# Transposes directly behind the next scores, and readers of matmul results one slot later, in a bucketed attention with a gated feed-forward

## The chip, the core and the metric

The kernel runs on one NeuronCore of a Trainium2 chip. Its engines work side by side: TensorE (PE for matmuls, PEld for the loads of their stationary operand), VectorE (DVE), ScalarE (ACT), GpSimd (POOL) and SyncE (SP), which issues the DMA transfers here. In the trace each of them runs its instructions in the order in which the program lists them, so one that has to wait holds up those behind it on its engine. The metric is the device time of one execution in microseconds (us).

## The reference

There are 4 batches, 8 heads, 768 positions and 64 elements per head. Each query and key gets a bucket from the signs of six projections, and a query attends only to keys of its own bucket. The outputs of the heads are laid side by side to 512 columns and go through a feed-forward with a causal convolution as gate.

```
q_bits = (np.einsum('bhsd,dk->bhsk', q, proj) > 0)      # keys alike
mask = q_bucket[:, :, :, None] == k_bucket[:, :, None, :]
scores = np.where(mask, scale * q @ k.T, -1e9)
attn = exp(scores - max) / sum;   x = attn @ v           # heads merged: B, S, 512
gate = sigmoid(sum_k conv_w[k] * xp[:, k:k + S, :])      # five taps
out = (gate * (x @ w_val)) @ w_out
```

## The kernel before

A unit is one head of one batch; there are 32. A unit has six tiles of 128 queries, so there are 192 tiles, and the main loop runs over them: slot `k` is one turn of that loop. The instruction order of TensorE, VectorE, ScalarE and GpSimd is the order of the code (`manual_schedule`).

A tile goes through the slots as a pipeline. `scores(k + 1)` in slot k multiplies the queries with all 768 keys (four matmuls, L266; the bucket comparison is part of the product through extra rows) into one of two pairs of PSUM banks, `s`. `maxima(k)`, `factors(k)` and `shifts(k)` on VectorE (L272, L278, L282) find the row's maximum and from it the scale and shift of the exponential. `exponentials(k)` on ScalarE (L290) writes `p` and the row's sum; it frees the banks that `scores(k + 2)` needs. In each even slot VectorE inverts the sums of two tiles (`row_sums`, `recip`), which waits for the exponential of the later one. `normalise(k - 2)` on GpSimd (L305) scales `p`. `transposes(k - 3)` turns it over in two halves of three matmuls each (L314) into two banks `tp`, and `keep_transposed` copies each half to SBUF as `pt` on ScalarE (L323), at the start of the next slot.

When the six tiles of a unit are done, `attn_v` multiplies them with the values into the single bank `av` (L337): two key blocks, that is four matmuls, in each odd slot, and so three odd slots for a unit. At its end ScalarE copies `av` to `x` (L345, two copies), and for every second unit `pair_x` splits `x` and runs the convolution's taps (L357 to L368). When a batch has its four pairs, four sigmoids follow (L372), and `moe` becomes the batch's feed-forward, a generator that the loop advances by about a step per slot. A step is four matmuls. Three steps fill one accumulator: either a `val` (L399), which VectorE multiplies with the gate (L404, `ht`) and then splits (L408, L410), or an `outp` (L424), which ScalarE or VectorE copies to `o` (L432, L430) for the output DMA. In the loop the accumulator is the single bank `m`; after the loop `tp` and `s` serve as well.

In the first third of the loop VectorE, ScalarE and GpSimd also convert the weights (L91 to L113), and TensorE computes bucket projections ahead (L204, L226), which VectorE reads at once (L207, L229).

In slot k TensorE's order is: scores of tile k + 1, a step of the feed-forward, bucket projections if any, value products if k is odd, transposes of tile k - 3. ScalarE's is: copies of the transposes of tile k - 4, exponential of tile k, then the readers of results that came in this slot.

Of the kernel before, what the change touches and what calls it, by code (L numbers as in the profile page):

```python
# [8 lines left out]
FP32 = mybir.dt.float32  # L9
FP32R = mybir.dt.float32r  # L10
AF = mybir.ActivationFunctionType
ALU = mybir.AluOpType
# [14 lines left out]
def kernel(  # L27
# [10 lines left out]
    nc = tc.nc  # L38
    B, H, _, S = qk.shape
    P = 128  # L40
    D = 64
    KB = S // P
    HS = S // 2
    NP = H // 2
    KW = 5
    LAG = 3
# [11 lines left out]
    xp = ctx.enter_context(tc.tile_pool(name="xp", bufs=2))  # L58
# [269 lines left out]
    def attn_v(i, pts):  # L328
        b, h = units[i]
        hh, c = h % 2, h // 2  # L330
        av = ps_v.tile([P, 512], FP32, name="av")
        vt = vts[i]
        for kb in range(KB):
            if kb:
                yield
            for s, pt in enumerate(pts):
                nc.tensor.matmul(out=av[s * D:(s + 1) * D, 0:HS], lhsT=vt[:, kb, hh * D:(hh + 1) * D], rhs=pt[kb // 3][:, kb % 3, :],  # L337
                                 start=(kb == 0), stop=(kb == KB - 1), tile_position=(0, s * D))
        if hh == 0:
            x = cur["x"] = xp.tile([P, S + KW - 1], FP32, name="x")  # L340
            nc.gpsimd.memset(x[:, 0:KW - 1], 0.0)
        x = cur["x"]
        for s in range(2):
            o = KW - 1 + s * HS
            nc.scalar.copy(out=x[hh * D:(hh + 1) * D, o:o + HS], in_=av[s * D:(s + 1) * D, 0:HS])  # L345
        if hh == 1:
            if c == 0:
                cur["xs"], cur["g"] = {}, []
            convs.append(pair_x(b, c, x, cur["g"], cur["xs"]))

    def pair_x(b, c, x, gs, xs_):
        for o in (0, HS):
# [21 lines left out]
            moes.append(moe(b, xs_, gs))  # L374

    def acc_tile():
        pools = accs
        pool, name = pools[0]
        pools.append(pools.pop(0))
        if name == "s":  # L380
            return pool.tile([P, 2, 512], FP32, name="s")[:, 0, :]
        return pool.tile([P, 512], FP32, name=name)

    def moe(b, xs_, g):
# [7 lines left out]
        def val(o, j):  # L392
            acc = acc_tile()
            m = 0
            for wi, xi in ((0, 0), (1, 0), (0, 1)):
                if m:
                    yield
                for c in range(NP):
                    nc.tensor.matmul(out=acc[:, 0:HS], lhsT=wv[wi][:, c, j * P:(j + 1) * P],  # L399
                                     rhs=xs_[(c, o)][xi], start=(m == 0), stop=(m == 11))  # L400
                    m += 1
                later()
            ht = hp.tile([P, HS], FP32, name="ht", bufs=2)
            nc.vector.tensor_tensor(out=ht, in0=acc[:, 0:HS], in1=g[j][:, o:o + HS], op=ALU.mult)  # L404

            def split():
                hh = hp.tile([P, HS], FP32R, name="hh")
                nc.vector.tensor_copy(out=hh, in_=ht)  # L408
                hl = hp.tile([P, HS], FP32R, name="hl")
                nc.gpsimd.tensor_tensor(out=hl, in0=ht, in1=hh.bitcast(FP32), op=ALU.subtract)  # L410
                hs[(o, j)] = (hh, hl)
            todo.append(split)
            yield

        def outp(o, tb):
            for gens in weights:
                finish(gens)
            acc = acc_tile()
            m = 0
            for hi, wi in ((0, 0), (0, 1), (1, 0)):  # L420
                if m:
                    yield
                for j in range(NP):
                    nc.tensor.matmul(out=acc, lhsT=hs[(o, j)][hi][:, tb * P:(tb + 1) * P],  # L424
                                     rhs=wo[wi][:, j, :], start=(m == 0), stop=(m == 11))
                    m += 1
                later()
            ob = op.tile([P, 512], FP32, name="o")
            if cur["gates"]:
                nc.vector.tensor_copy(out=ob, in_=acc)  # L430
            else:
                nc.scalar.copy(out=ob, in_=acc)  # L432
            r0 = o + tb * P
            nc.sync.dma_start(out=out[b, r0:r0 + P, :], in_=ob)
            yield

        def idle(n):
# [18 lines left out]
    tiles = [(i, qt) for i in range(len(units)) for qt in range(KB)]  # L456

    raws, stacks, vts, ss, nbs, ps, tps, sums, rcs, nms, gs, cur = {}, {}, {}, {}, {}, {}, {}, {}, {}, {}, {}, {}
    avs, convs, moes, early = [], [], [], {}
    accs = [(ps_m, "m")]  # L460

    def step(gens):
# [7 lines left out]
    def finish(gens):  # L470
        while gens:
            step(gens)
# [3 lines left out]
    with tc.manual_schedule(engines=ENGINES):  # L476
# [10 lines left out]
        step(weights[1])  # L487
        ahead = [early_bits()]
        turn = 0
        for k in range(N + LAG + 1):  # L490
            if 0 <= k - LAG - 1:
                keep_transposed(k - LAG - 1)
            pair = k % 2 == 0 and 0 <= k - 2 < N
            if k < N:
                maxima(k)
# [14 lines left out]
                scores(k + 1)  # L510
            if k < N:
                exponentials(k)
            if k >= 60 or k % 2:
                step(convs)
            for _ in range((1, 0, 2, 0, 2, 2)[k % 6]):
# [10 lines left out]
            if k % 2:  # L526
                step(avs)
                step(avs)
            if 0 <= k - LAG < N:
                transposes(k - LAG)  # L530
        accs[:] = [(ps_m, "m"), (ps_t, "tp"), (ps_s, "s"), (ps_t, "tp"), (ps_s, "s")]
        finish(avs)
        cur["gates"] = 0
        cur["end"] = True
        while convs:
# [62 lines left out]
```

## Time and profile before

| | |
|---|---|
| median of 3 runs | 622.93 us (622.74 to 623.79) |
| span of the profiled execution, first to last instruction | 620.8 us |
| instructions | 10648 |
| TensorE matmuls busy | 585.5 us, 94% |
| VectorE busy | 437.6 us, 70% |
| ScalarE busy | 421.4 us, 68% |
| GpSimd busy | 395.6 us, 64% |

The profiled execution is one run; its time is its span, and the runs' times are taken around it on the device, so that the median stands 2.1 us over the span. A busy share is a mean over the whole span, and stages with different limits are mixed in it. The matmuls are pipelined and their ends are modelled, so that two of them overlap in the listing.

### The profile page before, as it was taken

What the parts mean: (1) busy time and instruction counts of PE and PEld (TensorE: products, weight loads), DVE (VectorE), ACT (ScalarE), POOL (GpSimd) and SP (SyncE); (2) the same over time, 40 slices, a digit from 0 to 9 for tenths busy, and PEclk for the clock granted to TensorE, in tenths of its full rate; (3) what the DMA queues carried; (4) which work ended last, traced back from release to release, by engine and by line L of the source; (5) the groups of instructions that cost most, each with busy time, mean ns of one, the idle gap of its engine ahead of it and who ended that gap; (6) DMA issues with size and microseconds to landing.
All of it is one profiled execution on the core that took longest, in us unless ns stands there. A gap on an engine that the chain in (4) does not pass through costs nothing.

```text
span 620.8 us, 10648 instructions
## 1 busy us (share of the span) xinstructions
PE 585.5 (94%) x3496; PEld 423.4 (68%) x3496; DVE 437.6 (70%) x1017; ACT 421.4 (68%) x881; POOL 395.6 (64%) x373
## 2 busy tenths in 40 slices
PE   5789898989999999999999999999999999999997
PEld 2655565555657777776767777777667877775895
DVE  5869798998975866668575867569665877665532
ACT  2777777778778666777787676777787766765400
POOL 3576868778766765578564777568764777544321
PEclk9799999999999999999999999999999999999999
DMA  6467666564532235243433234333422213200111
GB/s 227 123 197 199 200 167 208 157 175 118 133 83 68 70 79 142 72 108 82 122 82 107 61 80 126 84 115 82 108 70 78 67 42 91 69 18 1 51 52 51
DMA packets 29031, 64.64 MB, mean 104 GB/s; under 512 B 4937, under 2 KB 10057, under 8 KB 28977
## 3 DMA queue, kind: packets, MB, share of 16 engines
q1 hardware_dynamic: 28832, 63.93, 37.8%
q8 instruction: 28, 0.46, 0.3%
q14 instruction: 27, 0.21, 0.1%
q10 hardware_dynamic: 144, 0.03, 0.0%
HBM read 30.60 MB, written 7.86 MB: 62 GB/s over the span
## 4 chain that ended last, share of the span: by engine, by line
PE 66%; DVE 12%; ACT 12%; DMA 5%; issue 3%; POOL 2%; SPq 1%; ACTq 0%; POOLq 0%; DVEq 0%
PE av L337 17%; PE s L266 16%; PE tp L314 12%; PE m L424 8%; PE m L399 7%; ACT p L290 5%; DVE nm L272 4%; ACT pt L323 3%; ACT x L345 2%; DMA w<-in_w_val_dram 2%; DVE g L368 2%; PE tp L399 1%; PE tp L424 1%; PE s L424 1%; DMA bk<-bq 1%
## 5 line engine op out<-in xcount | busy, mean ns | idle before, releaser
L305 POOL TENSOR_SCALAR p<-p,ri 128x768 f32<-128x768 f32 x192 | 210.5, 1100 | 156.0 <-DVE nb L282 130.8
L272 DVE TENSOR_REDUCE nm<-s 128x1 f32<-128x768 f32 x192 | 182.5, 950 | 61.2 <-PE s L266 61.0
L290 ACT ACTIVATE p<-s,nb,gs 128x768 f32<-128x768 f32 x192 | 192.6, 1003 | 46.2 <-DVE nb L282 41.9
L323 ACT COPY pt<-tp 128x384 f32<-128x384 f32 x384 | 165.7, 485 | 75.3 <-PE tp L314 74.4
L314 PEld LDWEIGHTS tp<-ident,p 128*128 128x128 f32 x1152 | 130.3, 142 | 72.2 <-issue 43.6
L314 PE MATMUL tp<-ident,p 128*128 128x128 f32 x1152 | 164.4, 279 | 2.6 <-ACT pt L323 2.1
L337 PE MATMUL av<-pt,vt 128*64 128x384 f32 x768 | 144.9, 498 | 0.0
L266 PE MATMUL s<-ak,aq 76*128 76x384 f32 x384 | 118.1, 389 | 23.2 <-ACT p L290 19.7
L266 PE MATMUL s<-bk,bq 128*128 128x384 f32 x384 | 101.3, 345 | 0.4 <-DVE bq L252 0.4
L337 PEld LDWEIGHTS av<-pt,vt 128*64 128x64 f32 x768 | 47.0, 136 | 61.5 <-issue 61.4
L266 PEld LDWEIGHTS s<-ak,aq 76*128 76x128 f32 x384 | 59.2, 194 | 38.7 <-ACT p L290 34.6
L368 DVE SCALAR_TENSOR_TENSOR g<-x,cw_sb,g 128x768 f32<-128x768 f32 x64 | 79.4, 1241 | 2.2 <-POOL g L366 2.1
L266 PEld LDWEIGHTS s<-bk,bq 128*128 128x128 f32 x384 | 71.7, 194 | 0.8 <-issue 0.8
L173 POOL TENSOR_TENSOR bq<-r,aq 128x768 fp32r<-128x768 f32 x31 | 59.2, 1909 | 0.1
L410 POOL TENSOR_TENSOR hl<-ht,hh 128x384 fp32r<-128x384 f32 x32 | 32.3, 1009 | 39.5 <-DVE hh L408 39.5
L345 ACT COPY x<-av 64x384 f32<-64x384 f32 x64 | 30.4, 475 | 29.7 <-PE av L337 29.0
L282 DVE TENSOR_SCALAR nb<-nm,gs 128x1 f32<-128x1 f32 x192 | 40.4, 211 | 3.5
L399 PE MATMUL m<-xh,wv 128*128 128x384 f32 x200 | 42.7, 337 | 0.0
L358 POOL TENSOR_TENSOR xl<-x,xh 128x384 fp32r<-128x384 f32 x32 | 33.4, 1059 | 13.8 <-DVE xh L357 13.8
L290 ACT ACTIVATION_READ_ACCUMULATOR p<-s,nb,gs 128x1 f32 x192 | 39.0, 203 | 0.0
L404 DVE TENSOR_TENSOR ht<-m,g 128x384 f32<-128x384 f32 x25 | 13.9, 556 | 35.6 <-PE m L399 29.2
L424 PE MATMUL m<-wo,hh 128*128 128x512 f32 x144 | 38.1, 394 | 0.0
(86 smaller groups left out, 486.9 us busy)
## 6 DMA issues: line engine op xcount, KB each, us to landing
r<-in_qk_dram SPq DMA_DIRECT2D x32, 384.0 KB
vt<-in_v_dram SPq DMA_DIRECT2D x16, 384.0 KB
out_dram<-o SPq DMA_DIRECT2D x24, 256.0 KB
ak<-aq SPq DMA_DIRECT2D x31, 192.0 KB
bk<-aq SPq DMA_DIRECT2D x31, 192.0 KB
bk<-bq SPq DMA_DIRECT2D x31, 192.0 KB
bq<-aq SPq DMA_DIRECT2D x31, 192.0 KB
hh<-in_qk_dram SPq DMA_DIRECT2D x16, 192.0 KB
```

The source lines that it names most:

```text
L173: nc.gpsimd.tensor_tensor(out=bq, in0=r, in1=aq.bitcast(FP32), op=ALU.subtract)
L266: nc.tensor.matmul(out=s[:, hf, 0:HS], lhsT=lq[0:n, qs], rhs=rk[0:n, hf * HS:(hf + 1) * HS], start=n == M, stop=n == P)
L272: nc.vector.tensor_reduce(out=nm, in_=s[:, :, 0:HS], axis=AX.XY, op=ALU.max, negate=True)
L290: nc.scalar.activation(out=p, in_=s[:, :, 0:HS], func=AF.Exp, bias=nb, scale=gs.pop(k), accum_out=sm[:, k % 2, 0:1])
L305: nc.gpsimd.tensor_scalar(out=p, in0=p, scalar1=rcs.pop(k), scalar2=1.0, op0=ALU.mult, op1=ALU.mult)
L314: nc.tensor.transpose(out=tp[:, n * P:(n + 1) * P], in_=p[:, kb * P:(kb + 1) * P], identity=ident)
L323: nc.scalar.copy(out=pt[:, :, qo:qo + P], in_=tp[:, 0:HS].rearrange("p (a b) -> p a b", b=P))
L337: nc.tensor.matmul(out=av[s * D:(s + 1) * D, 0:HS], lhsT=vt[:, kb, hh * D:(hh + 1) * D], rhs=pt[kb // 3][:, kb % 3, :], start=(kb == 0), s ...
L345: nc.scalar.copy(out=x[hh * D:(hh + 1) * D, o:o + HS], in_=av[s * D:(s + 1) * D, 0:HS])
L368: nc.vector.scalar_tensor_tensor(out=g, in0=x[:, k:k + S], scalar=w, in1=g, op0=ALU.mult, op1=ALU.add)
L399: nc.tensor.matmul(out=acc[:, 0:HS], lhsT=wv[wi][:, c, j * P:(j + 1) * P], rhs=xs_[(c, o)][xi], start=(m == 0), stop=(m == 11))
L424: nc.tensor.matmul(out=acc, lhsT=hs[(o, j)][hi][:, tb * P:(tb + 1) * P], rhs=wo[wi][:, j, :], start=(m == 0), stop=(m == 11))
```

## The change

The copy of `av` to `x`, the gating of a `val` and the store of an `outp` become closures. They are put on a list, `readers`, which is emptied in the next slot right after the exponential of that slot, or when the next accumulator is taken; after the loop they run at once. The transposes move from the end of the slot to the place behind the exponential in the code, which on TensorE is directly behind the scores, and their copies follow in the same slot. The loop is one slot shorter.

```diff
--- before.py
+++ after.py
@@ -336,17 +336,29 @@
             for s, pt in enumerate(pts):
                 nc.tensor.matmul(out=av[s * D:(s + 1) * D, 0:HS], lhsT=vt[:, kb, hh * D:(hh + 1) * D], rhs=pt[kb // 3][:, kb % 3, :],
                                  start=(kb == 0), stop=(kb == KB - 1), tile_position=(0, s * D))
-        if hh == 0:
-            x = cur["x"] = xp.tile([P, S + KW - 1], FP32, name="x")
-            nc.gpsimd.memset(x[:, 0:KW - 1], 0.0)
-        x = cur["x"]
-        for s in range(2):
-            o = KW - 1 + s * HS
-            nc.scalar.copy(out=x[hh * D:(hh + 1) * D, o:o + HS], in_=av[s * D:(s + 1) * D, 0:HS])
-        if hh == 1:
-            if c == 0:
-                cur["xs"], cur["g"] = {}, []
-            convs.append(pair_x(b, c, x, cur["g"], cur["xs"]))
+
+        def take():
+            if hh == 0:
+                x = cur["x"] = xp.tile([P, S + KW - 1], FP32, name="x")
+                nc.gpsimd.memset(x[:, 0:KW - 1], 0.0)
+            x = cur["x"]
+            for s in range(2):
+                o = KW - 1 + s * HS
+                nc.scalar.copy(out=x[hh * D:(hh + 1) * D, o:o + HS], in_=av[s * D:(s + 1) * D, 0:HS])
+            if hh == 1:
+                if c == 0:
+                    cur["xs"], cur["g"] = {}, []
+                convs.append(pair_x(b, c, x, cur["g"], cur["xs"]))
+        soon(take)
+
+    def soon(f):
+        readers.append(f)
+        if cur["end"]:
+            read()
+
+    def read():
+        while readers:
+            readers.pop(0)()
 
     def pair_x(b, c, x, gs, xs_):
         for o in (0, HS):
@@ -374,6 +386,7 @@
             moes.append(moe(b, xs_, gs))
 
     def acc_tile():
+        read()
         pools = accs
         pool, name = pools[0]
         pools.append(pools.pop(0))
@@ -401,7 +414,10 @@
                     m += 1
                 later()
             ht = hp.tile([P, HS], FP32, name="ht", bufs=2)
-            nc.vector.tensor_tensor(out=ht, in0=acc[:, 0:HS], in1=g[j][:, o:o + HS], op=ALU.mult)
+
+            def gate():
+                nc.vector.tensor_tensor(out=ht, in0=acc[:, 0:HS], in1=g[j][:, o:o + HS], op=ALU.mult)
+                todo.append(split)
 
             def split():
                 hh = hp.tile([P, HS], FP32R, name="hh")
@@ -409,7 +425,7 @@
                 hl = hp.tile([P, HS], FP32R, name="hl")
                 nc.gpsimd.tensor_tensor(out=hl, in0=ht, in1=hh.bitcast(FP32), op=ALU.subtract)
                 hs[(o, j)] = (hh, hl)
-            todo.append(split)
+            soon(gate)
             yield
 
         def outp(o, tb):
@@ -425,13 +441,16 @@
                                      rhs=wo[wi][:, j, :], start=(m == 0), stop=(m == 11))
                     m += 1
                 later()
-            ob = op.tile([P, 512], FP32, name="o")
-            if cur["gates"]:
-                nc.vector.tensor_copy(out=ob, in_=acc)
-            else:
-                nc.scalar.copy(out=ob, in_=acc)
-            r0 = o + tb * P
-            nc.sync.dma_start(out=out[b, r0:r0 + P, :], in_=ob)
+
+            def store():
+                ob = op.tile([P, 512], FP32, name="o")
+                if cur["gates"]:
+                    nc.vector.tensor_copy(out=ob, in_=acc)
+                else:
+                    nc.scalar.copy(out=ob, in_=acc)
+                r0 = o + tb * P
+                nc.sync.dma_start(out=out[b, r0:r0 + P, :], in_=ob)
+            soon(store)
             yield
 
         def idle(n):
@@ -456,7 +475,7 @@
     tiles = [(i, qt) for i in range(len(units)) for qt in range(KB)]
 
     raws, stacks, vts, ss, nbs, ps, tps, sums, rcs, nms, gs, cur = {}, {}, {}, {}, {}, {}, {}, {}, {}, {}, {}, {}
-    avs, convs, moes, early = [], [], [], {}
+    avs, convs, moes, early, readers = [], [], [], {}, []
     accs = [(ps_m, "m")]
 
     def step(gens):
@@ -487,9 +506,7 @@
         step(weights[1])
         ahead = [early_bits()]
         turn = 0
-        for k in range(N + LAG + 1):
-            if 0 <= k - LAG - 1:
-                keep_transposed(k - LAG - 1)
+        for k in range(N + LAG):
             pair = k % 2 == 0 and 0 <= k - 2 < N
             if k < N:
                 maxima(k)
@@ -510,6 +527,10 @@
                 scores(k + 1)
             if k < N:
                 exponentials(k)
+            read()
+            if 0 <= k - LAG < N:
+                transposes(k - LAG)
+                keep_transposed(k - LAG)
             if k >= 60 or k % 2:
                 step(convs)
             for _ in range((1, 0, 2, 0, 2, 2)[k % 6]):
@@ -526,10 +547,9 @@
             if k % 2:
                 step(avs)
                 step(avs)
-            if 0 <= k - LAG < N:
-                transposes(k - LAG)
         accs[:] = [(ps_m, "m"), (ps_t, "tp"), (ps_s, "s"), (ps_t, "tp"), (ps_s, "s")]
         finish(avs)
+        read()
         cur["gates"] = 0
         cur["end"] = True
         while convs:
```

On TensorE, in the feed-forward of the first batch (`s` scores, `tp` transposes, `m` the accumulator: `wo` and `hl` an output group, `wv` and `xh` a value group, `av` value products), the rows before are:

```order
L266 MATMUL s<-ak,aq 128x384 x2
L266 MATMUL s<-bk,bq 128x384 x2
L424 MATMUL m<-wo_122,hl 128x512 x4
L314 MATMUL tp<-ident,p 128x128 x6
L266 MATMUL s<-ak,aq 128x384 x2
L266 MATMUL s<-bk,bq 128x384 x2
L399 MATMUL m<-xh,wv_120 128x384 x4
L337 MATMUL av<-pt,vt 64x384 x4
L314 MATMUL tp<-ident,p 128x128 x6
```

In the changed kernel, at the same scores:

```order
L266 MATMUL s<-ak,aq 128x384 x2
L266 MATMUL s<-bk,bq 128x384 x2
L314 MATMUL tp<-ident,p 128x128 x6
L440 MATMUL m<-wo_122,hl 128x512 x4
L266 MATMUL s<-ak,aq 128x384 x2
L266 MATMUL s<-bk,bq 128x384 x2
L314 MATMUL tp<-ident,p 128x128 x6
L412 MATMUL m<-xh,wv_120 128x384 x4
L337 MATMUL av<-pt,vt 64x384 x4
```

The six transposes moved ahead of the feed-forward group and of the value products; in an odd slot the value products now stand directly ahead of the next scores.

On ScalarE, around the end of unit 16 (`p` the exponential, `x` the copies of the value product, `pt` the copies of the transposes, `o` the store of an output group), before:

```order
L290 ACTIVATE p,sm<-s,nb,gs 128x768
L345 COPY x<-av 64x384 x2
L323 COPY pt<-tp 128x3x128 x2
L290 ACTIVATE p,sm<-s,nb,gs 128x768
L432 COPY o<-m 128x512
L323 COPY pt<-tp 128x3x128 x2
L290 ACTIVATE p,sm<-s,nb,gs 128x768
```

In the changed kernel, from the same exponential on:

```order
L290 ACTIVATE p,sm<-s,nb,gs 128x768
L323 COPY pt<-tp 128x3x128 x2
L290 ACTIVATE p,sm<-s,nb,gs 128x768
L347 COPY x<-av 64x384 x2
L323 COPY pt<-tp 128x3x128 x2
L290 ACTIVATE p,sm<-s,nb,gs 128x768
L450 COPY o<-m 128x512
L323 COPY pt<-tp 128x3x128 x2
L290 ACTIVATE p,sm<-s,nb,gs 128x768
```

The order of exponentials and copies of transposes is as it was; the copies to `x` and to `o` stand one exponential later.

## Rows read from the trace of the kernel before

**Rows 1.** The page's head.

```profile
span 620.8 us, 10648 instructions
```

**Rows 2.** Stretches: length, busy us (instructions) by engine, TensorE's clock, DMA share, GB/s.

```profile
38.00:187.00 149.00, 135.45 (x868) 85.07 (x868) 130.62 (x297) 112.30 (x242) 113.27 (x104) 1.00 0.58 161
187.00:560.00 373.00, 367.72 (x2217) 274.81 (x2216) 254.28 (x615) 275.01 (x576) 246.07 (x233) 1.00 0.33 84
560.00:621.00 61.00, 55.63 (x288) 44.88 (x286) 26.02 (x42) 13.20 (x25) 17.02 (x17) 0.99 0.10 39
```

**Rows 3.** Waits, whole span: us in total, times, longest us.

```profile
ACT pt L323 <- PE tp L314: 74.4, 95, 2.1
...
PEld s L266 <- ACT p L290: 34.6, 47, 2.1
...
DVE ht L404 <- PE m L399: 29.2, 18, 3.0
```

**Rows 4.** One of these waits, from 38 to 187 and from 187 to 560 us.

```profile
PEld s L266 <- ACT p L290: 17.5, 21, 2.1
...
PEld s L266 <- ACT p L290: 9.3, 20, 1.1
```

**Rows 5.** The chain that ended last, 280 to 320 us: start, us, what.

```profile
282.68 0.70 PE s L266 x4
...
284.07 0.66 PE tp L314 x6
...
286.87 0.81 PE tp L314 x6
...
289.93 0.96 PE s L266 x4
290.89 1.44 PE av L337 x8
292.33 0.49 PE tp L314 x3
...
292.84 0.35 ACT pt L323
...
293.70 0.99 ACT p L290 x2
...
294.74 0.96 PE s L266 x4
```

**Rows 6.** Groups by line and form: busy, mean ns; idle before, releaser.

```profile
L345 ACT COPY x<-av 64x384 f32<-64x384 f32 x64 | 30.4, 475 | 29.7 <-PE av L337 29.0
...
L229 DVE TENSOR_SCALAR ht<-m,packed 128x384 fp32r<-128x384 f32 x8 | 5.4, 676 | 4.3 <-PE m L226 4.2
```

**Rows 7.** A stretch of the first third, columns as in rows 2.

```profile
88.00:105.00 17.00, 15.05 (x98) 9.76 (x96) 16.46 (x36) 11.89 (x25) 12.55 (x12) 1.00 0.68 196
```

**Rows 8.** Timeline, 244 to 256 us: start, us, what.

```profile
249.88 1.09 PE L424 MATMUL m<-wo,hl 128*128 128x512 f32 x4
250.08 0.96 DVE L272 TENSOR_REDUCE nm<-s 128x1 f32<-128x768 f32 x1 [1.57 <-PE s L266]
...
250.81 0.82 PE L314 MATMUL tp<-ident,p 128*128 128x128 f32 x6
251.01 0.59 ACT L432 COPY o<-m 128x512 f32<-128x512 f32 x1
...
251.26 0.22 DVE L282 TENSOR_SCALAR nb<-nm,gs 128x1 f32<-128x1 f32 x1
...
251.49 0.87 ACT L323 COPY pt<-tp 128x384 f32<-128x384 f32 x2
...
252.17 0.86 PE L399 MATMUL m<-xh,wv 128*128 128x384 f32 x4
252.24 1.02 ACT L290 ACTIVATE p<-s,nb,gs 128x768 f32<-128x768 f32 x1
...
253.12 0.22 ACT L290 ACTIVATION_READ_ACCUMULATOR p<-s,nb,gs 128x1 f32 x1
```

## The prediction

> **What bounds the kernel now.** I read the busy time by stretch first [rows 2]. From 187 to 560 us TensorE is busy for 367.72 of 373.00 us; there the kernel is near the end of what its matmuls allow. From 38 to 187 us it is busy for 135.45 of 149.00 us, and VectorE for 130.62: two engines are nearly full and neither quite. TensorE is the engine to shorten, but its idle time lies mainly in the first third.
>
> Next, the waits [rows 3]. The weight load of a score matmul waits for the exponential 47 times, 34.6 us in total. That is the one wait of weight on TensorE. It counts more than matmul idle time would, because it runs from the moment the load could have begun, while earlier matmuls still drain. Split by stretch it is 17.5 us before 187 us and 9.3 us from there to 560 [rows 4]; the rest, 7.8 us by difference, is start-up. The 74.4 us that ScalarE waits for transposes [rows 3] shows why: a late transpose makes a late copy, and the next exponential stands behind that copy in ScalarE's queue.
>
> The chain of work shows one such turn [rows 5]. The scores end, four value-product matmuls follow (1.44 us), then the first half of the transposes (0.49), the copies (0.86, from 292.84 to 293.70), the exponential (0.99), and only then the scores at 294.74, whose bank that exponential frees. From 289.93 to 294.74 is 4.81 us for two slots. The same matmuls without a wait are two score groups at 0.70, transposes once after a value product at 0.81 and once elsewhere at 0.66, and 1.44: 4.31 us. This turn loses 0.50 us.
>
> **What the change does, and its price.** No instruction is added or removed but for which engine stores a few results. In the slot, transposes now follow the scores at once, and the feed-forward and value-product matmuls come after them. Copies of transposes keep their place between two exponentials, but their data is there 1.44 us earlier where a value product was in front, and 0.93 us earlier where an output group of the feed-forward was (249.88 to 250.81, [rows 8]). The chain above loses its link from value product to transposes.
>
> What then sets an exponential? VectorE: from the start of the maximum at 250.08 to the end of the shift at 251.48 is 1.40 us [rows 8], and the exponential with its accumulator read takes 1.10 (252.24 to 253.34). ScalarE must do this and the copies, 0.86 us, each slot: 1.96, so 3.92 us for two slots, and every sixth slot adds two copies of 0.475 us [rows 6], 0.32 us per two slots. That is 4.24, just below the 4.31 that the matmuls need. So ScalarE is no bound, but in the slots without feed-forward work it has only 0.07 us to spare.
>
> Gain at the start: of 7.8 us I take 3 (nothing to 7.8), because the first slots also wait for loads and first weights.
>
> Gain from 38 to 187 us: the wait is 17.5 us, but VectorE allows less. In its fullest stretch, 88 to 105 us, it is busy for 16.46 of 17.00 us, 97% [rows 7]; at that share its 130.62 us need 134.9, so at most 14.1 of the 149 us can go, and from 88 to 105 nothing. I take 10, nearer the upper bound, since VectorE has slack in most of the other stretches.
>
> A cost in the same stretch: bucket projections now follow the transposes, 0.66 us later, and VectorE waits for them in its queue with the next maximum behind. There are 8 such reads for the early pass [rows 6] and as many for the others; 16 by 0.66 is 10.6 us if each counts, nothing if none. Only where VectorE is nearly full does it count: 2 us.
>
> Gain from 187 to 560: all 9.3 us of the waits may go. Against it stands a new wait. The accumulator of the feed-forward has one bank, and its reader now stands a slot later, behind the next exponential. In the slot at 249.88 [rows 8] the last group runs, the copy follows at 251.01, and the next group starts at 252.17. In the changed order the transposes come ahead of that group, so it would start near 252.83. Had the exponential stayed at 252.24, the copy would end at 253.34 + 0.59 = 253.93: 1.1 us too late. But the exponential starts at 252.24 only because the copies at 251.49 stand in front, and their transposes now come 0.93 us sooner. Copies from about 250.9 to 251.76, exponential to 252.86, copy to 253.45: 0.6 us too late. Where a value product lies between, 1.44 us hide this. Some 15 results are stored in the loop, about 8 of them without that cover: 5 us, and 1 for those near the sigmoids, where ScalarE is held longer. The results that VectorE gates wait for no exponential and have its 1.40 us path ahead, about as long as the transposes and the group together; they now find their sum finished (VectorE waited 29.2 us for it, [rows 3]), so I price them at nothing. Net gain 3 (from a loss of 7, 15 by 1.1 less 9.3, to a gain of 9.3).
>
> Boundaries between matmuls: transposes after a value product take 0.81 against 0.66 [rows 5], 0.15 us more, 96 times: 14.4 us that go. In their place, scores follow the value product 96 times. The trace has no such pair. At best they take the 0.70 they take after transposes; at worst the 0.96 of a start after a wait, 96 by 0.26 is 25.0 us. Net from -14.4 to +10.6. I take the middle of these prices, the same 0.15 us, since it is the same preceding matmul: nothing.
>
> A rule of the Trainium skill speaks against this middle. "TensorE: Matmul & The Clock Gate", Part 3 (the mechanism), says that a weight load overlaps running matmuls only if it goes to other row groups; scores after a value product would then pay their load in full, as after a wait, and the sum would be the 10.6 us worse. This trace agrees only in part: the score group that follows full-width transposes takes 0.70 us, so its load is hidden there.
>
> Moving the output DMAs a slot later, on SyncE's queue, costs nothing: they are not waited for until the end, where reads are immediate again. From 560 us on, TensorE works on feed-forward groups in the same order as before [rows 2]; I count nothing there.
>
> Sum: 3 + 10 - 2 + 3 = 14 us. The profiled span is 620.8 [rows 1], which the median of the runs, 622.93, exceeds by 2.1 us. 606.8 + 2.1 gives **609 us**.
>
> **The rivals.** *All waits go.* 7.8 + 14.1 + 9.3 = 31.2 us at most, 592; with start-up and the new bank waits at half their prices, some 24: 599. For it: normalised tiles stand ready well before their new place, since POOL is busy for only 113.27 of 149 us [rows 2]. Against it: VectorE's share.
>
> *Exposed weight loads,* the rule above: at the boundary price of 10.6 us the kernel takes 620; halfway, 614.
>
> *Slower: the one bank.* Place: the first matmul of each feed-forward accumulation, which waits in TensorE's queue for the reader of the one before, with value products and the next scores behind it. Some 37 accumulations run in the loop by the program's order, 22 gated and 15 stored. The gains before this cost are 3 + 10 - 2 + 9.3 = 20.3 us, so the change is no gain from 0.55 us for each, and at 1.1 us it costs 40.7: 643; at 0.8, 632. For it: in the slot above an unmoved exponential gives exactly 1.1. Against it: gates wait for no exponential, and value products cover every other store.
>
> *No effect:* the first third is bound by VectorE, so the waits only change their name there, and the loop's 3 us are lost to the bank: 622 to 624.
>
> **How the numbers follow.** Forecast (603 to 614): 0.52. All waits go (592 to 602): 0.17. Exposed loads (615 to 621): 0.16. No effect: 0.05. Slower: 0.10. A change of 0.2%, 1.2 us, is about what a measurement of this kernel can tell from none. Faster is 0.52 + 0.17 + 0.16 = 0.85, same 0.05, slower 0.10. The range leaves out the slower cases, the cases of no effect and the lower end of the second case: 598 to 621.
>
> **What would show it right or wrong.** Right: the weight load of scores no longer waits 34.6 us for the exponential but under 12; ScalarE's waits for transposes and for value products fall to a few us; VectorE is busy for over 92% from the early value products to the first sigmoid; the loop's last two thirds change little. Wrong in size: a wait of the feed-forward matmul for the copy of its predecessor of over 10 us in total, or score groups after value products at 0.9 us or more. Wrong altogether: transposes that wait for normalised tiles or for copies, tens of times.

## The result and the profile after

The changed kernel takes 631.78 us (median of 4 runs, 630.70 to 632.90), the kernel before 622.84 beside it: 1.0145 of it, with a 95% interval of 1.0122 to 1.0169. It is slower by 9 us where the forecast was 14 us faster, and it lies outside the range.

The page of the changed kernel has this head and these busy times (as [rows 1]):

```profile
span 628.9 us, 10651 instructions
PE 589.3 (94%) x3496; PEld 429.4 (68%) x3496; DVE 437.6 (70%) x1015; ACT 422.7 (67%) x883; POOL 392.6 (62%) x373
```

The work is the same; VectorE is busy for 437.6 us in both. So the time went into waiting. Where it went is read from the start of the same work in both traces. The first score matmul of tile 66 starts at 187.5 us in the kernel before (first row) and at 192.0 in the changed one (second row):

```profile
L266 PE MATMUL s<-ak,aq x2: 337/388/440, 187.5 to 187.8; 76*128 76x384 f32 x2
```
```profile
L266 PE MATMUL s<-ak,aq x2: 337/388/440, 192.0 to 192.3; 76*128 76x384 f32 x2
```

That is 4.5 us lost by then. Tile 12 had started 0.6 us earlier (37.6 against 38.2), so the stretch from tile 12 to tile 66, the first third below, itself lost 5.1. From tile 66 to tile 186 another 3.9 us are lost (359.6 us against 355.7), and what follows takes 77.3 us against 77.6. The same stretches as in [rows 2], moved by these shifts:

```profile
38.00:192.00 154.00, 137.23 (x868) 87.82 (x866) 130.03 (x297) 110.87 (x242) 113.82 (x104) 0.99 0.55 156
192.00:569.00 377.00, 369.89 (x2219) 277.02 (x2220) 255.62 (x613) 278.19 (x579) 242.21 (x233) 1.00 0.32 83
569.00:629.00 60.00, 55.34 (x283) 45.43 (x281) 25.18 (x42) 12.18 (x22) 17.11 (x17) 1.00 0.11 40
```

VectorE did not become fuller in the first third: 130.03 of 154 us, 84%, where it had 130.62 of 149. The waits over the whole span, with the rows that answer to [rows 3] among them:

```profile
ACT p L290 <- DVE nb L282: 105.6, 127, 6.0
...
PEld s L266 <- ACT p L290: 52.2, 57, 2.1
ACT pt L323 <- PE tp L314: 41.3, 51, 2.0
...
PEld s L266 <- ACT pt L323: 24.7, 40, 1.2
DVE xh L369 <- ACT x L347: 24.1, 12, 5.8
...
DVE ht L229 <- PE m L226: 8.8, 5, 2.6
...
DVE ht L419 <- PE m L412: 2.3, 2, 1.4
```

Some waits went as intended: ScalarE waits for transposes for 41.3 us instead of 74.4, and the gate's 29.2 us are 2.3. But the one that was to go, the scores' weight load behind the exponential, grew from 34.6 to 52.2 us. (The row with 24.7 us is new, but it is idle time of the weight loads; no score matmul waits for these copies.) The first row names the reason: the exponential now waits 105.6 us for VectorE's shift. The same row of the kernel before:

```profile
ACT p L290 <- DVE nb L282: 41.9, 54, 6.0
```

By stretch, as [rows 4], 38 to 192 us and then 192 to 569:

```profile
PEld s L266 <- ACT p L290: 26.6, 25, 2.1
...
PEld s L266 <- ACT p L290: 17.8, 26, 1.3
```

The chain that ended last, by engine, on the page of the kernel before and on that of the changed one:

```profile
PE 66%; DVE 12%; ACT 12%; DMA 5%; issue 3%; POOL 2%; SPq 1%; ACTq 0%; POOLq 0%; DVEq 0%
```
```profile
PE 64%; DVE 19%; ACT 7%; DMA 4%; issue 4%; POOL 2%; SPq 0%; ACTq 0%; POOLq 0%; DVEq 0%
```

ScalarE's part falls from some 74 to 44 us, as the change would have it, and VectorE's rises from some 74 to 119.

### The profile page after: what moved, and what is told of

It is laid out like the page before. It is cut to its first block, busy times and chain, and to the rows that moved or that the text cites. A ratio compares the mean times of both kernels' runs of the same rounds, so it can differ in the third digit from the quotient of the medians.

```text
span 628.9 us, 10651 instructions
## 1 busy us (share of the span) xinstructions
PE 589.3 (94%) x3496; PEld 429.4 (68%) x3496; DVE 437.6 (70%) x1015; ACT 422.7 (67%) x883; POOL 392.6 (62%) x373
## 3 DMA queue, kind: packets, MB, share of 16 engines
q1 hardware_dynamic: 28832, 63.93, 37.1%
## 4 chain that ended last, share of the span: by engine, by line
PE 64%; DVE 19%; ACT 7%; DMA 4%; issue 4%; POOL 2%; SPq 0%; ACTq 0%; POOLq 0%; DVEq 0%
PE s L266 16%; PE av L337 15%; PE tp L314 12%; PE m L412 8%; DVE nm L272 7%; PE m L440 6%; ACT p L290 4%; DVE g L380 3%; DMA w<-in_w_val_dram 2%; DVE nb L282 1%; PE tp L412 1%; PE tp L440 1%; PE s L440 1%; DVE gs L278 1%; PE s L412 1%
## 5 line engine op out<-in xcount | busy, mean ns | idle before, releaser
L305 POOL TENSOR_SCALAR p<-p,ri 128x768 f32<-128x768 f32 x192 | 207.9, 1085 | 143.2 <-DVE nb L282 135.6
L290 ACT ACTIVATE p<-s,nb,gs 128x768 f32<-128x768 f32 x192 | 191.1, 995 | 110.6 <-DVE nb L282 105.6
L323 ACT COPY pt<-tp 128x384 f32<-128x384 f32 x384 | 164.8, 483 | 42.2 <-PE tp L314 41.3
L314 PE MATMUL tp<-ident,p 128*128 128x128 f32 x1152 | 159.1, 274 | 2.5 <-ACT pt L323 1.1
L314 PEld LDWEIGHTS tp<-ident,p 128*128 128x128 f32 x1152 | 137.0, 141 | 14.1 <-POOL p L305 3.2
L266 PE MATMUL s<-ak,aq 76*128 76x384 f32 x384 | 115.3, 381 | 25.6 <-ACT p L290 23.6
L266 PEld LDWEIGHTS s<-ak,aq 76*128 76x128 f32 x384 | 62.5, 192 | 100.1 <-ACT p L290 52.2
L412 PE MATMUL m<-xh,wv 128*128 128x384 f32 x200 | 46.7, 357 | 1.2 <-ACT o L450 1.2
L440 PE MATMUL m<-wo,hh 128*128 128x512 f32 x144 | 40.4, 410 | 0.6 <-ACT o L450 0.6
L369 DVE CAST xh<-x 128x384 fp32r<-128x384 f32 x32 | 20.9, 663 | 25.7 <-ACT x L347 24.1
L290 ACT ACTIVATION_READ_ACCUMULATOR p<-s,nb,gs 128x1 f32 x192 | 37.4, 195 | 0.0
## 6 DMA issues: line engine op xcount, KB each, us to landing
ak<-aq SPq DMA_DIRECT2D x31, 192.0 KB
bk<-aq SPq DMA_DIRECT2D x31, 192.0 KB
bk<-bq SPq DMA_DIRECT2D x31, 192.0 KB
bq<-aq SPq DMA_DIRECT2D x31, 192.0 KB
hh<-in_qk_dram SPq DMA_DIRECT2D x16, 192.0 KB
```

Of the source, the lines that this page charges most:

```text
L266: nc.tensor.matmul(out=s[:, hf, 0:HS], lhsT=lq[0:n, qs], rhs=rk[0:n, hf * HS:(hf + 1) * HS], start=n == M, stop=n == P)
L290: nc.scalar.activation(out=p, in_=s[:, :, 0:HS], func=AF.Exp, bias=nb, scale=gs.pop(k), accum_out=sm[:, k % 2, 0:1])
L305: nc.gpsimd.tensor_scalar(out=p, in0=p, scalar1=rcs.pop(k), scalar2=1.0, op0=ALU.mult, op1=ALU.mult)
L314: nc.tensor.transpose(out=tp[:, n * P:(n + 1) * P], in_=p[:, kb * P:(kb + 1) * P], identity=ident)
L323: nc.scalar.copy(out=pt[:, :, qo:qo + P], in_=tp[:, 0:HS].rearrange("p (a b) -> p a b", b=P))
```

## The experiments

Three theories run through the expectations. By one (T), the early transposes make the loss. By another (R), the late readers do, since they hold the banks of `m` and `av` for longer. By the third (V), the exponential really waited for VectorE's path from the maximum to the shift; ScalarE's copies only stood last in front of it, so taking them away shows the next wait, and everything that now comes later to VectorE's queue costs. The boundaries between matmuls on TensorE and the clock (B) are the smaller suspects. Each kernel was timed beside the kernel before, whose medians there were 622.2 to 622.5 us.

**One part alone.** The transposes and their copies moved, the readers at once as before:

```diff
     def soon(f):
-        readers.append(f)
-        if cur["end"]:
-            read()
+        f()
```

> The transposes and their copies moved as in the change; the readers of value products and feed-forward results stay in their own slot. Theory R (the late readers cost: copies to x now stand ahead of the copies of transposes, VectorE waits for them with the next maximum behind, stores hold the one bank): the loss goes and some of the gain comes, 614 to 621 us. Theory T (the transposes cost: score loads behind value products, projections later, VectorE as the next link of the chain): as slow as the whole change, 629 to 634 us.

Measured: 633.15 us, 1.0174 [1.0152, 1.0196]. The moved transposes cost 11 us by themselves, and T's number holds. ScalarE's wait for transposes is down to 23.8 us, and the exponential waits 103.1 us for the shift: V's picture as well.

The other part alone, readers late, transposes at the end of the slot and their copies in the next:

```diff
...
-            if 0 <= k - LAG < N:
-                transposes(k - LAG)
-                keep_transposed(k - LAG)
...
+            if 0 <= k - LAG < N:
+                transposes(k - LAG)
```

> The readers a slot later as in the change; transposes stay at the end of the slot and their copies at the start of the next. Theory R: slower than before, 627 to 633 us. Theory T: no change or a little faster, 619 to 624 us, since VectorE no longer waits for the sums.

Measured: 652.14 us, 1.0477 [1.0448, 1.0505]: 30 us more than the kernel before, far outside both expected ranges. Its waits:

```profile
ACT pt L323 <- PE tp L314: 126.9, 118, 3.2
...
DVE xh L369 <- ACT x L347: 44.6, 12, 7.1
...
PEld m L440 <- ACT o L450: 10.1, 6, 1.7
```

ScalarE waits even longer for transposes, VectorE longer for `x`, and the accumulator's bank is held. Together the two parts cost 9 us, not 41: with early transposes, the late readers are harmless; without them they are not. So neither part can be charged by itself, and neither T nor R tells the whole.

All of the change, but the readers behind the copies of the transposes:

```diff
-            read()
             if 0 <= k - LAG < N:
                 transposes(k - LAG)
                 keep_transposed(k - LAG)
+            read()
```

> The whole change, but on ScalarE the late readers stand behind the copies of the transposes instead of ahead of them. Theory R in its part on order: the transposes no longer wait for copies behind x, 2 to 5 us faster than the change, 627 to 630 us, unless the stores, now later still, hold the accumulator's bank longer. Theory T: within 1 us of the change, 631 to 633 us.

Measured: 659.51 us, 1.0616 [1.0566, 1.0667]. Neither range holds: the place of the readers within ScalarE's slot matters by 28 us. VectorE's wait for `x` is 47.9 us here (24.1 in the changed kernel), and the weight loads of the accumulations wait 15.6 us for the copies to `o` (3.7 there).

The change with only the copies to `x` late (gates and stores at once), and the change with only these at once:

```diff
-            soon(gate)
+            gate()
...
-            soon(store)
+            store()
```

> The whole change, but gates and stores of the feed-forward stay in their own slot; only the copies to x come a slot later. If the one accumulator bank held longer is what the loop's last two thirds lose (output groups that wait for the store before them, 0.45 us each): about 4 us faster than the change, 627 to 629 us. If it is the copies to x, or the transposes: within 1 us of the change, 631 to 633 us.

```diff
-        soon(take)
+        take()
```

> The whole change, but the copies to x stay in their own slot; gates and stores come late, transposes early. If the late copies to x are what costs and the late gates and stores what gains (only x late was 10 us slower than transposes alone, and the whole change 11 us faster than only x late): 619 to 624 us, about the kernel before. If the parts do not add up, because the late copies need the other readers late: within 2 us of the change, 630 to 634.

Measured: 643.24 us, 1.0323 [1.0285, 1.0361], where neither expected time came, and 633.43 us, 1.0164 [1.0124, 1.0204], as if the parts did not add up. With gates and stores at once VectorE waits 36.0 us for value groups that now stand behind the transposes, and the exponential 135.0 us for the shift. That late gates and stores take 11 us of this away fits V, though no run parts the two; that late copies to `x` cost 10 us beside early gates (against the first kernel of this section) and nothing beside late ones is an interaction that I did not settle.

One piece on the kernel before: only the gate a slot later.

```diff
...
-            nc.vector.tensor_tensor(out=ht, in0=acc[:, 0:HS], in1=g[j][:, o:o + HS], op=ALU.mult)
+            def gate():
+                nc.vector.tensor_tensor(out=ht, in0=acc[:, 0:HS], in1=g[j][:, o:o + HS], op=ALU.mult)
+                todo.append(split)
...
-            todo.append(split)
+            soon(gate)
...
```

> The kernel before, with one piece of the change alone: the gate of a value group stands behind the next slot's shift on VectorE; transposes, copies of av and stores stay as they were. If VectorE's path from maximum to shift is what decides, this takes a wait out of VectorE's queue (29.2 us of waits for the accumulator before) at no cost to the order of TensorE: 617 to 621. If a late reader costs by itself because the single bank of the accumulator is held longer, as in the run with all readers late (652): 625 or more. If VectorE's waits were idle time that nobody missed: 622 to 624.

Measured: 623.31 us, 1.0015 [1.0000, 1.0031]. The 29.2 us that VectorE waited for value groups are 1.5 here, and the time did not fall: nobody had missed them.

**Which stretch.** The change from slot 66 on, and the change up to slot 65 (`now` chooses the order of the kernel before; the second kernel has `k < 66`):

```diff
-        if cur["end"]:
+        if cur["end"] or cur["now"]:
             read()
...
+            cur["now"] = 0 if k >= 66 else 1
...
-            if 0 <= k - LAG < N:
+            if 0 <= k - LAG < N and not cur["now"]:
                 transposes(k - LAG)
                 keep_transposed(k - LAG)
...
+            if 0 <= k - LAG < N and cur["now"]:
+                transposes(k - LAG)
```

> The whole change from slot 66 on; up to there transposes, copies and readers stand as in the kernel before. If the loss comes piece by piece in both stretches, as the starts of the scores say (about 4.5 us by 192 us, 4 after it), this takes 626 to 628. If the loss is mainly the clock's dip at 131 us and the late bucket projections, both of the first third, it takes 622 to 624. If the two stretches are tied by work that the first hands on, 630 to 632.

> The whole change up to slot 65; from there on the order of the kernel before. If the loss comes piece by piece: 626 to 628, the first third's 4.5 us alone. If the first third's loss comes back later, when the feed-forward has less left to wait for: 622 to 625. If the loss of the first third is what makes the later one: 630 or more.

Measured: 625.44 us, 1.0055 [1.0039, 1.0072], and 628.27 us, 1.0103 [1.0084, 1.0122]. That is 3.0 and 5.8 us, 8.8 in sum against 9.0 for the whole. Both lie just outside their ranges, but the sum says that the two stretches lose separately; what each loses by is for the next runs.

**VectorE's load.** Both kernels without four of the convolution's five taps (they leave out part of the result, to see what VectorE's time is worth):

```diff
-            else:
-                nc.vector.scalar_tensor_tensor(out=g, in0=x[:, k:k + S], scalar=w, in1=g, op0=ALU.mult, op1=ALU.add)
```

> The kernel before with four of the five convolution taps left out (64 instructions of VectorE, 79 us of its work); only the first tap remains. It is the base for the next run. Theory V (VectorE's queue sets the exponential in the first third and in the slots without feed-forward work): faster than the kernel before by up to 15 us, 608 to 618 us, since the scores' waits for the exponential also end sooner here. Theory B (the boundaries between matmuls and the clock decide, VectorE is not in the way): within 4 us of 622.

> The changed kernel with the same four taps left out, against the run of the kernel before without them. Theory V: the order of the change now gains, 5 to 12 us below that run, and the weight load's wait for the exponential falls under 20 us. Theory B: still 5 to 11 us above it.

Measured: 617.97 us and 618.29 us. With less work on VectorE the change costs nothing on balance; with it, 9 us. The taps are worth 4.5 us to the kernel before and 13.5 to the changed one. So most of the loss needs VectorE's work, which is V's claim. (Without taps the gates are also ready sooner; these runs do not part that from VectorE's queue.) The gain of 5 to 12 us that I expected did not come, and the weight load still waits 46.3 us for the exponential, not under 20. The page of the changed kernel without taps:

```profile
PE 70%; DVE 11%; ACT 10%; issue 3%; DMA 2%; POOL 2%; SPq 0%; ACTq 0%; POOLq 0%; DVEq 0%
```

The balance hides two sides. At tile 12 the changed kernel stands 2.4 us behind (39.5 us against 37.1), and its clock is at half from 30 to 37 us, where the other's is not. From there to tile 66 it gains 0.9 us, where with taps it lost 5.1, and from tile 66 to tile 186 another 1.0. In the second stretch some units gain 4.6 us together, the one from tile 96 most (13.68 against 15.35), and others lose 3.6. Those that lose are nearly all the ones with late stores, and they lose the same with the taps and without: the unit from tile 132 takes 19.15 instead of 18.61 us in both pairs. The wait behind it is there too:

```profile
PEld m L410 <- ACT o L448: 2.5, 5, 0.7
```

So with room on VectorE the early transposes do gain a few microseconds; the late stores, which need nothing of VectorE's work, take most of that back.

**The projections.** The whole change, but the early bucket projections ahead of the transposes on TensorE; VectorE's reads keep their place:

```diff
...
             read()
+            if 6 <= k < 60 and k % 6 in (2, 4):
+                step(ahead)
             if 0 <= k - LAG < N:
                 transposes(k - LAG)
...
```

> The whole change, with the matmuls of the early projections put between the scores and the transposes, as near to the scores as in the kernel before; VectorE's reads of them keep their place. Theory V: VectorE's waits for them fall from 8.8 to about 4 us, and as VectorE is in the chain there, the time falls by 3 to 5 us, 627 to 629. Theory B: no change, 631 to 633.

Measured: 628.37 us (10 runs, 625.17 to 631.23), 1.0087 [1.0060, 1.0113]: 3.4 us back, as V had it, and VectorE's wait for these projections is 3.6 us instead of 8.8. In its trace tile 66 starts at 187.9 us, within 0.4 of the kernel before. The chain shows what this undoes; the same place in the kernel before and in the changed one:

```profile
110.75 0.96 PE s L266 x4
111.72 1.44 PE av L337 x8
113.16 0.81 PE tp L314 x6
113.96 0.71 PE s L266 x4
114.67 0.85 PE m L204 x8
115.52 0.03 issue
115.55 0.68 DVE u L207
```
```profile
111.57 0.97 PE s L266 x4
112.55 0.66 PE tp L314 x6
113.20 1.44 PE av L337 x8
114.64 0.90 PE s L266 x4
115.55 0.66 PE tp L314 x6
116.20 0.88 PE m L204 x8
117.08 0.03 issue
117.11 0.68 DVE u L207
```

From the first scores to VectorE's read it is 4.80 us before and 5.54 after: six more transposes (0.66 us) stand between the scores and the projections. VectorE's maximum comes behind this read, the shift behind that, and with it the exponential.

**The order of value products and transposes.** The whole change, with the value products of odd slots ahead of the transposes:

```diff
             read()
+            if k % 2:
+                step(avs)
+                step(avs)
             if 0 <= k - LAG < N:
                 transposes(k - LAG)
...
-            if k % 2:
-                step(avs)
-                step(avs)
```

> The whole change, but in odd slots the four value products stand between the scores and the transposes. The pair of value products with scores behind them goes, and with it about 0.06 us per two slots by the gaps that I read (av to tp 1.02 against av to s 1.05 and tp to av 1.23); transposes come 1.44 us later in odd slots. If the early transposes are worth nothing, since VectorE sets the exponential, while the boundaries cost 5 us: 626 to 629. If the transposes' early place still counts for something: 632 to 640, towards the kernel with readers late and transposes at the end (652).

Measured: 639.45 us, 1.0295 [1.0263, 1.0327]. That is in the second range. Whatever the pairs of matmuls give back, the kernel loses 7.7 us more than the changed one to transposes that come 1.44 us later, with late readers behind them. ScalarE waits 87.1 us for them (41.3 in the changed kernel). So the boundaries between matmuls are not what the change loses by.

**The late stores.** After 192 us, the time from one unit's first scores to the next is longer by about 0.5 us where a unit computes six output groups, and in the one behind it where the last is stored (from tile 132 19.15 against 18.61 us, from tile 138 16.62 against 16.09; so from 78, 162 and 180), and elsewhere mostly the same. On TensorE of the changed kernel:

```profile
337.70 0.81 PE L314 MATMUL tp<-ident,p 128*128 128x128 f32 x6
338.77 0.96 PE L412 MATMUL m<-xh,wv 128*128 128x384 f32 x4 [0.26 <-ACT o L450]
```

and on its ScalarE, where the copy that holds the bank `m` stands behind the exponential:

```profile
337.14 1.01 ACT L290 ACTIVATE p<-s,nb,gs 128x768 f32<-128x768 f32 x1
338.03 0.21 ACT L290 ACTIVATION_READ_ACCUMULATOR p<-s,nb,gs 128x1 f32 x1
338.12 0.60 ACT L450 COPY o<-m 128x512 f32<-128x512 f32 x1
```

The next accumulation starts 1.07 us after its transposes began. So three kernels have VectorE copy the stores in the loop: the whole change, the one with the projections ahead, and the kernel before.

```diff
-                if cur["gates"]:
+                if cur["gates"] or not cur["end"]:
                     nc.vector.tensor_copy(out=ob, in_=acc)
```

> The whole change, but in the loop VectorE instead of ScalarE copies a finished output group (the store keeps its late place, and there it waits for no exponential). If the one bank of the accumulator, held until ScalarE's copy behind the exponential, makes the loss after 192 us (eight times some 0.45 us): 627.5 to 629.5. If that loss comes from the boundaries between matmuls or from VectorE's path, this adds 14 copies to VectorE and gains nothing: 631 to 634.

> Both repairs: bucket projections ahead of the transposes, and the late stores on VectorE. If the two losses are apart from each other and these are their causes, 624 to 625.5 (628.4 with the projections ahead, less 3 to 4): nearly all of the 9 us back. If either was only covering for VectorE: 627 or more.

> The control: the kernel before with its stores on VectorE in the loop, at their old place. If who copies does not matter where the reader stands at once: 622 to 624; if the copies weigh on VectorE's queue: 624 to 628; if they were a burden to ScalarE before: below 621.

Measured: 629.12 us, 1.0098 [1.0065, 1.0131]; 626.11 us, 1.0050 [1.0030, 1.0070]; and 623.41 us, 1.0018 [1.0004, 1.0032]. In the one with both repairs the same accumulation follows its transposes by 0.57 us:

```profile
335.70 0.82 PE L317 MATMUL tp<-ident,p 128*128 128x128 f32 x6
336.27 0.96 PE L415 MATMUL m<-xh,wv 128*128 128x384 f32 x4
```

That is 0.50 us for this store, and the waits for the copy are gone. From tile 66 to tile 186 this kernel takes 357.0 us, where the changed one takes 359.6 and the kernel before 355.7. So the repair gives back 2.6 of the 3.9 us; the control takes 356.2, so that the copies on VectorE seem to cost some 0.5 themselves. By the medians the repairs give back 2.7 and 5.7 of 9 us. The interval of the first still touches that of the changed kernel, so for the bank alone the stretch and the next run say more. The second stands 0.6 us above what I expected, and its trace has two stretches of half the clock in the first third, 10.2 us in all.

Last, the change from slot 66 on, with the stores on VectorE, so that the late projections play no part:

```diff
...
+            cur["now"] = 0 if k >= 66 else 1
...
-                if cur["gates"]:
+                if cur["gates"] or not cur["end"]:
...
```

> The change from slot 66 on, with its late stores on VectorE. If the causes add up (3.0 us for the change after the first third, of which the one bank is 2.6), this is within 1.2 us of the kernel before: 621.5 to 623.7. If the early transposes were worth something once the bank is out of the way: below 621. If something else after slot 66 costs, VectorE's path above all: 624.5 or more.

Measured: 623.14 us (12 runs), 1.0013 [0.9999, 1.0027]. Against the same kernel with ScalarE's stores (625.44) that is 2.3 us back, with intervals that do not touch: the bank's cost is shown. With both costs out of the way the change is worth nothing that can be measured. No version here that computes the whole result beats the kernel before.

## Why the prediction was wrong

**The step that failed** is the reading of the wait behind its two gains, 10 us from 38 to 187 us and 9.3 from there to 560. The scores' weight load waited for the exponential, and I took the copies of the transposes to be what held the exponential, on the strength of one turn of the chain [rows 5]. That turn was typical of the later stretch only. In the chain of the kernel before, read from 38 to 110 and from 110 to 187 us, the copies of the transposes have 4 pieces with 2.6 us, too little for the sums by line:

```profile
by line: DMA w<-in_w_val_dram 17.0%; DVE nm L272 9.6%; issue 7.3%; DMA w<-in_w_out_dram 7.2%; DMA bk<-bq 7.0%; POOL bq L173 5.7%; DMA hl<-in_qk_dram 4.4%; PE av L337 4.1%; PE s L266 3.7%; DVE g L368 3.4%; DVE o L94 3.3%; ACT p L290 3.0%; AC
```
```profile
by line: DVE nm L272 15.8%; PE s L266 12.1%; PE av L337 11.2%; DVE g L368 9.2%; ACT p L290 9.0%; PE tp L314 5.9%; issue 5.0%; DVE nb L282 3.4%; DVE ht L229 3.4%; PE m L226 3.4%; DVE u L207 3.3%; DVE w L97 2.9%; DVE gs L278 2.6%; PE m L204 2
```

VectorE's pieces sum to 58 us, those of the transfers to some 22. There was no 10 us to win there. In the later stretch the copies did stand in the chain, with 4.2% of it, 16 us, as its sum by line from 187 to 560 us shows; behind it the same from 192 to 568 in the changed kernel:

```profile
by line: PE av L337 23.3%; PE s L266 21.4%; PE tp L314 17.3%; PE m L424 11.2%; PE m L399 9.7%; ACT p L290 5.9%; ACT pt L323 4.2%; ACT x L345 2.9%; issue 1.3%; ACT g L372 0.7%; DVE g L368 0.5%; DVE nm L272 0.5%; ACT L372 0.3%; ACT L290 0.3%;
```
```profile
by line: PE s L266 20.8%; PE av L337 19.6%; PE tp L314 15.2%; PE m L412 11.8%; PE m L440 8.2%; DVE nm L272 5.1%; ACT p L290 3.6%; DVE g L380 3.5%; issue 3.1%; ACT x L347 1.2%; DVE nb L282 1.1%; ACT o L450 1.0%; DVE xh L369 0.9%; ACT pt L323
```

The copies nearly left the chain (under 0.9%), and VectorE's maximum and taps, 1.0% of it before, have 8.6% now. The wait moved to the next link, which was nearly as long; without the taps, some units of this stretch did get faster. In the sum's terms: the start gave 0.6 us for 3, the first third lost 5.1 where 10 less 2 were to come, and the later stretch lost 3.9 where 3 were to come. I had named VectorE as what sets the exponential, with its 1.40 us path, and then counted only its busy share (97%) as a bound. By these runs it is not the share that binds but the order of its queue: maximum, shift, taps, conversions and reads of projections follow each other, and one late operand shifts all behind it. At 84% busy it held the kernel back more than at 88% before. In the chain of the changed first third VectorE's pieces sum to 57 us, as before; TensorE's rise from 34 to 51, which fits operands that come later to VectorE.

**Start-up, 3 us.** Mis-sized: tile 12 started 0.6 us earlier, and that is within what kernels with the start of before differ by (36.7 to 39.3 us).

**Projections, -2 us.** The mechanism held, the size did not. With them ahead of the transposes tile 66 starts 4.1 us earlier, knock-on effects included; each of the two traces has one such stretch of half the clock, 3.4 us, in the first third (last section). At 10.2 us of half the clock each, the kernel with both repairs takes 153.3 us from tile 12 to tile 66, the one with the stores alone 156.8: 3.6 us. So the clock does not make this difference. It, some 4 us, and the clock's dip, up to 1.6, cover the 5.1 us of the first third. VectorE's wait for the early ones rose from 4.2 [rows 6] to 8.8 us; the longest, 2.6 us, comes right behind the dip.

**The one bank, 6 us.** The mechanism held; the size did not. I had 8 stores at 0.6 and 1; TensorE waits eight times for the copy, and the runs show 2.3 to 2.6 us in total, net of what the repair costs.

**Boundaries, nothing.** In the sum this held within its bounds: six tiles with value groups and no stores take 17.29 us from tile 120 and 17.47 before. The price of a pair was a little low: scores after a value product take 0.90 in the chain above, 0.20 more than the 0.70 after transposes where I had taken 0.15, and nearer the 0.97 of a start after a wait. It reaches my sign of 0.9 us for being wrong in size. The rule that I had weighed, in the Trainium skill ("TensorE: Matmul & The Clock Gate", Part 3, the mechanism), is that a weight load overlaps running matmuls only if it goes to other row groups; this trace comes near it behind value products, and not behind transposes (0.70). What made it harmless is that the transposes behind these scores take 0.66 instead of 0.81, so a pair loses some 0.05 by the chain's rows, about 5 us for 96 at most, and the units' times do not show even that.

**The rest of the loss.** From tile 66 to tile 186, 1.3 us remain with the stores repaired. The units from tiles 108 and 144 take 1.1 and 1.3 us more than before, others a little less. Without taps the one from 144 takes 15.17 us instead of 16.65 in the changed order, so VectorE is the likely cause; no run singles it out, and this stays open.

**The rivals and the signs.** The slower rival had one of the causes, the bank, but with 2.6 us where it needed 20.3 to decide; that its 632 at 0.8 us for each accumulation is close to the measured time is luck. "No effect" had the other, a first third bound by VectorE so that waits only change their name, at a chance of 0.05. Of the signs that I named, the weight load's wait grew, ScalarE's waits fell only halfway, VectorE's share sank to 84%, and transposes waited for normalised tiles only 8 times, 3.2 us.

## What to carry to other kernels

A wait names what came last, not what would come last without it. Before pricing its removal, follow the chain of work stretch by stretch and ask which path to the same instruction is the next longest; if it is nearly as long, the removal gives next to nothing, and only the costs of the move remain. An engine that runs its queue in order can bind by what stands in it one behind the other, so a reader there whose operand comes later delays the critical instruction behind it, here at 84% busy. Where a result sits in a single bank, ask what stands ahead of its reader in its engine's queue: here an exponential did, and each such store cost the next accumulation some 0.5 us. And two kernels with the same time need not be alike: compare them unit by unit, since a gain in some can hide a loss in others.

## What the hardware showed unexpectedly

TensorE's granted clock fell to half, its 1.2 GHz level, for some 3.5 us at 131 us in the changed kernel; the profiled run of the kernel before has nothing like it between its start-up and its last microsecond. In the 6.3 us before the fall TensorE had been busy for 3.94. The stretch, and the value products in it, which elsewhere take 1.51 us in this listing:

```profile
131.30:134.80 3.50, 3.50 (x13) 1.21 (x11) 3.37 (x10) 2.13 (x5) 2.94 (x3) 0.51 0.32 67
```
```profile
132.07 2.83 PE L337 MATMUL av<-pt,vt 128*64 128x384 f32 x8
```

That and the slower transposes beside them (1.13 us for 0.82) took 1.6 us longer. All 11 profiles of kernels with the taps and a changed first third have such a stretch near 78 us or between 128 and 135 us, or both, some of 6.8 us; of the 5 with the order of before in the first third, 2 have one, near 129. It goes with the spread of the runs: of the kernel with the projections ahead, the fastest run (625.17 us) has a mean granted clock of 0.997, the four slowest (630.10 to 631.23) 0.980 to 0.985. What brings a stretch on is not settled here.
